# Block-sparse attention on one core: all steps in one hand-written order, sampled blocks from a packed table, V tiles held per pair, keys read in place

## The chip, the cores and the metric

The kernel runs on one core of a Trainium2 chip. The metric is device time of one execution, in microseconds (us). Engine names are those of the profile: PE is TensorE, PEld its weight loads, DVE is VectorE, ACT is ScalarE, POOL is GpSimd, SP is the engine whose queue issues all DMAs of this kernel.

## The reference

Attention over 4 batches of 8 heads, 768 positions of 64 numbers, with a mask in blocks of 32 positions (24 blocks), followed by a feed-forward layer with a clipped quadratic in place of a relu:

```python
scores = (1/sqrt(64)) * q @ k.T                  # per batch and head, 768 x 768
mask = |block(i) - block(j)| <= 1                # a band of three blocks
mask |= block(i) in (0, 23) | block(j) in (0, 23)    # first and last block see all and are seen by all
mask |= block(j) in sampled_blocks[block(i)]     # three blocks drawn per block of queries
attn = softmax(where(mask, scores, -1e9)) @ v
x = attn as (3072 tokens, 512)
h = x @ w_in                                     # 2048 columns
g = where(h >= 1, h, where(h <= -1, 0, (h + 1)**2 / 4))
out = g @ w_out
```

The sampled blocks are an input (64-bit integers), so which keys and values a block needs is known only on the chip. The two weights come as 64-bit floats and are converted on the chip.

## The kernel before

**Attention.** Two heads form a pair; there are 16 pairs, four for each batch. A pair has four rounds, a round eight blocks of queries. The first round scores the two global blocks (0 and 23) against all keys, the second adds the six blocks beside them, the third and fourth take eight blocks each. A block other than 0 and 23 needs 256 keys: the band of 96, the two global blocks (64), and three sampled ones (96). `gather_k` (L201) and `gather_k_sampled` (L212) copy these 256 columns of K into a tile `kg` on GpSimd: three wide copies a round for ends and bands, and one copy of 32 columns per sampled block (L218), 66 in a pair, each at an address from a register. `gather_v` (L221) does the same for V by DMA: three to four DMAs for the fixed blocks of each half of a round, and one DMA per sampled block (L240), again 66 in a pair, into a tile `vg`. The addresses come from two tables in SBUF (`k_at`, `v_at`); `offsets` (L113) reads the nine or twelve values that half a round needs into registers (L114), once on GpSimd for K and once on SP for V. A block that is sampled twice or already inside the band is pointed at 32 rows of zeros behind V.

**A round's steps.** `scores` (16 matmuls of 32 x 256, K of 64 rows, eight array tiles side by side), `top` (row maxima, DVE), `top_scale`, `expo` (ACT), `turn` (four transposes for each of the two heads, into one PSUM bank `t`), `turn_copy` (DVE for the first head, ACT for the second), `values` (16 matmuls of 128 rows x 32 for each head, 65 columns: 64 of V and a column of ones that sums the weights), `norm`. After the third and the fourth round three 128 x 128 tiles of the result are transposed (`x_turn`, L353) and split into a high and a low part (`x_hi`, `x_lo`). The round of the global blocks is scored first and finished inside the second one.

**Feed-forward.** `moe` (L398) works on 384 tokens, half a batch, at a time: 16 slices of 128 hidden columns each. A slice is 12 matmuls of 384 columns into the one bank `h` (`l1`, L421 to L423: three products of high and low parts for each of four pairs), then `g_relu`, `g_sq` (ACT), `g_max` (DVE), `g_hi` (ACT), `g_lo` (DVE), and nine matmuls of 512 columns (`l2`, L449 to L451). `h` is free for the next slice when `g_max` has read it. The second weight lies converted in DRAM and is loaded once per slice (L405). The feed-forward of batch b stands beside the attention of batch b + 1; that of the last batch has only its own tail beside it.

**Conversion.** `convert` turns 1 MB of 64-bit weights into two 32-bit parts: two DMAs into `raw`, one ACT and four DVE instructions on `cva`, then the split on ACT and DVE. Eight of these are needed for the first weight before the feed-forward can use it, eight more run during the first half-batch.

**Order.** Each step is entered into a list with a planned time (`at`); the list is sorted and called through at the end. Planned times are numbers in no unit that the chip knows: a pair of the first batch starts every `TP0` = 24 of them, a later one every `TP` = 48, a slice takes 6, and the table `P` holds how far before or after its round each step stands. The layer that records the instructions then lets an engine take instructions of different steps out of this order; so single matmuls of `values` stand between those of `l1` in the program. An engine runs its own instructions in the program's order. SP's DMAs stand in one queue, and each waits there until its target buffer is free.

```python
for k in range(n):
    for x in range(NR):
        Q_V.dma_start(out=vg[32 * x + 32:32 * x + 64, k0 + k, 1], in_=v_ext[b, j, bass.ds(at_[k * NR + x], BLK)])
```

## Time and profile before

| | |
|---|---|
| median of three runs | 1312.4 us (1311.61 to 1315.64) |
| profiled execution | 1320.8 us, of which the span of its instructions 1319.0 us |
| TensorE, matmuls | 1033.8 us busy (78%) |
| VectorE | 427.0 us (32%) |
| ScalarE | 412.4 us (31%) |
| GpSimd | 247.6 us (19%) |
| DMA | 157.89 MB in 155,837 packets, mean 120 GB/s |
| mean granted TensorE clock | 0.855 |

A matmul's busy time counts its way through the array, and matmuls follow each other before that ends, so 78% is not the share of TensorE's power that is used; what a stretch of matmuls costs is read from start to start. Issues of DMAs and register instructions are not counted as busy: SP has no row in the table, and its load is read from its queue.

### The profile page before, as it was taken

The page shows a single profiled execution, that of the slowest core. Times are in us where ns is not written, and L with a number is a line of the kernel's source. Part 1 is how long each engine was busy: PE and PEld are TensorE (multiplying, and loading weights), DVE is VectorE, ACT ScalarE, POOL GpSimd, SP SyncE. Part 2 cuts the span into 40 slices and gives each one's busy share as a digit, 9 for nine tenths or more (in the row PEclk, how much of TensorE's full clock was granted, in tenths as well). Part 3 has the DMA queues.
Part 4 walks back from the last instruction along what each step waited for, and adds up shares of the span by engine and source line. Part 5 has one row for each costly group of instructions (what it writes and reads, how often), then busy time and mean ns, then how long its engine had stood idle before and what let it go on. Part 6 is the DMA issues. An engine that isn't in the chain of part 4 may idle for free.

```text
span 1319.0 us, 26978 instructions
## 1 busy us (share of the span) xinstructions
PE 1033.8 (78%) x8928; PEld 742.6 (56%) x8928; DVE 427.0 (32%) x879; ACT 412.4 (31%) x800; POOL 247.6 (19%) x1205
## 2 busy tenths in 40 slices
...
GB/s 132 51 142 51 140 81 93 99 127 125 145 105 133 133 102 163 93 130 114 126 142 106 111 150 118 89 155 84 119 146 105 136 129 115 112 133 169 137 143 104
DMA packets 155837, 157.89 MB, mean 120 GB/s; under 512 B 25523, under 2 KB 128052, under 8 KB 155700
## 3 DMA queue, kind: packets, MB, share of 16 engines
...
q14 instruction: 65, 0.53, 0.1%
...
## 4 chain that ended last, share of the span: by engine, by line
SPq 44%; PE 29%; DMA 10%; issue 10%; DVE 4%; ACT 2%; POOL 1%; POOLq 0%; DVEq 0%; ACTq 0%
SPq L240 24%; SPq L114 10%; PE oa L449 5%; PE oa L450 4%; PE oa L451 4%; DMA w<-wo_dram 3%; PE h L421 3%; DMA raw<-in_moe_w_in_dram 3%; DMA vg<-in_v_ext_dram 3%; PE h L423 3%; PE h L422 3%; PE s L264 2%; SPq L231 2%; SPq L229 2%; SPq L234 2%
## 5 line engine op out<-in xcount | busy, mean ns | idle before, releaser
L421 PE MATMUL h<-x,wi 128*128 128x384 f32 x448 | 169.2, 378 | 59.1 <-DVE r L433 58.8
L218 POOL COPY kg<-k 128x32 f32 x1056 | 178.3, 222 | 124.9 <-issue 124.3
L449 PE MATMUL oa<-w,gh 128*128 128x512 f32 x384 | 166.5, 446 | 21.7 <-DMA w<-wo_dram 15.5
L319 PE MATMUL o<-vg,pt 128*32 128x65 f32 x2464 | 122.4, 256 | 66.6 <-DMA vg<-in_v_ext_dram 66.2
L76 ACT CAST gh<-r 128x384 fp32r<-128x384 f32 x128 | 65.6, 513 | 324.0 <-PE oa L450 298.7
L207 POOL COPY kg<-k 128x512 f32<-128x512 f32 (+1 forms) x48 | 29.1, 606 | 731.1 <-DMA k<-in_qk_t_dram 714.8
L450 PE MATMUL oa<-w,gh 128*128 128x512 f32 x384 | 162.5, 423 | 1.2 <-DVE w L161 1.2
L422 PE MATMUL h<-x,wi 128*128 128x384 f32 x448 | 161.5, 360 | 0.0
L451 PE MATMUL oa<-w,gl 128*128 128x512 f32 x384 | 161.1, 420 | 0.0
L423 PE MATMUL h<-x,wi 128*128 128x384 f32 x448 | 158.3, 353 | 0.0
L319 PEld LDWEIGHTS o<-vg,pt 128*32 128x32 f32 x2464 | 77.5, 127 | 134.0 <-issue 94.8
L421 PEld LDWEIGHTS h<-x,wi 128*128 128x128 f32 x448 | 87.4, 195 | 90.9 <-DVE r L433 77.2
L264 PE MATMUL s<-kg,q 64*32 64x256 f32 x1184 | 109.6, 430 | 30.7 <-POOL kg L218 15.0
L442 DVE TENSOR_TENSOR gl<-r,gh 128x384 fp32r<-128x384 f32 x128 | 71.4, 558 | 169.1 <-ACT gh L76 148.8
L433 DVE SCALAR_TENSOR_TENSOR r<-r,h 128x384 f32<-128x384 f32 x112 | 61.8, 552 | 162.2 <-ACT r L430 161.8
L301 PE MATMUL t<-idf,p 128*128 128x128 f32 x464 | 86.4, 312 | 32.9 <-DVE pt L305 11.8
L427 ACT ACTIVATE r<-h,half_c 128x384 f32<-128x384 f32 x112 | 65.1, 581 | 140.7 <-PE h L423 134.9
L449 PEld LDWEIGHTS oa<-w,gh 128*128 128x128 f32 x384 | 78.4, 207 | 46.8 <-DMA w<-wo_dram 20.9
L275 DVE TENSOR_REDUCE m<-s 128x2 f32<-128x512 f32 x80 | 53.6, 687 | 150.6 <-PE s L264 150.6
L301 PEld LDWEIGHTS t<-idf,p 128*128 128x128 f32 x464 | 59.8, 157 | 58.0 <-DVE pt L305 19.2
L422 PEld LDWEIGHTS h<-x,wi 128*128 128x128 f32 x448 | 88.0, 196 | 4.7
L450 PEld LDWEIGHTS oa<-w,gh 128*128 128x128 f32 x384 | 80.3, 209 | 17.9 <-DVE w L161 3.4
...
## 6 DMA issues: line engine op xcount, KB each, us to landing
w<-wo_dram SPq DMA_DIRECT2D x112, 512.0 KB, 3.6
vg<-in_v_ext_dram SPq DMA_DIRECT2D x1088, 16.2 KB, 1.7
...
vg<-in_v_ext_dram SPq DMA_DIRECT2D x128, 65.0 KB, 3.0
raw<-in_moe_w_in_dram SPq DMA_DIRECT2D x16, 512.0 KB, 4.8
raw<-in_moe_w_out_dram SPq DMA_DIRECT2D x16, 512.0 KB, 5.3
wo_dram<-w SPq DMA_DIRECT2D x16, 512.0 KB, 6.8
...
```

The source lines that it names most:

```text
L114: _, vals = nc.values_load_multi_w_load_instructions(table[:, i0 - 1:i0 - 1 + n].rearrange("a i r -> a (i r)"), engines=[engine], min_val= ...
L218: nc.gpsimd.tensor_copy(out=kg[:, k0 + k, 160 + 32 * a:192 + 32 * a], in_=kt[:, bass.ds(at_[k * NR + a], BLK)])
L240: Q_V.dma_start(out=vg[32 * x + 32:32 * x + 64, k0 + k, 1], in_=v_ext[b, j, bass.ds(at_[k * NR + x], BLK)])
L264: nc.tensor.matmul(out=st["s", r, e][32 * w:32 * w + 32, 256 * g:256 * g + 256], lhsT=st["q"][es, i * BLK:(i + 1) * BLK], rhs=rhs, start=T ...
L301: nc.tensor.transpose(out=t[:, c * 128:(c + 1) * 128], in_=st["p", r, e][:, c * 128:(c + 1) * 128], identity=idf)
L319: nc.tensor.matmul(out=o[32 * w:32 * w + 32, e, gd], lhsT=st["pt", r, e][:, k:k + 32], rhs=rhs, start=start, stop=stop)
L421: nc.tensor.matmul(out=hv, lhsT=wi[:, j, 0, fs], rhs=x[:, 0], start=(j == 0), stop=False)
L422: nc.tensor.matmul(out=hv, lhsT=wi[:, j, 0, fs], rhs=x[:, 1], start=False, stop=False)
L423: nc.tensor.matmul(out=hv, lhsT=wi[:, j, 1, fs], rhs=x[:, 0], start=False, stop=(j == NP - 1))
L449: nc.tensor.matmul(out=o, lhsT=gh[:, ts], rhs=w[:, 0], start=(fi == 0), stop=False)
L450: nc.tensor.matmul(out=o, lhsT=gh[:, ts], rhs=w[:, 1], start=False, stop=False)
L451: nc.tensor.matmul(out=o, lhsT=gl[:, ts], rhs=w[:, 0], start=False, stop=(fi == NF - 1))
```

## The change

- **Table.** The three sampled blocks of a query block are packed into one number of 15 bits (`pack`, `kv_at`). Each engine that needs it reads it once for the whole kernel (`blocks`: 22 values on SP, 22 on VectorE, 44 on GpSimd) and keeps it in registers; a field is taken out by register arithmetic at each use (`field`). `offsets` goes.
- **V.** Per pair a tile `va` holds the band and one global block for every query block, loaded by five DMAs (`load_va`); it serves all rounds. The second half of the 256 rows is `vb`, per round: two or three DMAs for the other global block, and the sampled blocks. Of the three sampled blocks the first is fetched by a DMA on SP and the other two are copied from `va` by GpSimd (`gather_v_sampled`); in the first batch's first three rounds SP fetches two and GpSimd copies one.
- **K.** Band and ends are no longer copied. `scores` reads them in place, with three matmuls of 96, 64 and 96 columns per query block and head where there was one of 256. Only the sampled 96 columns are gathered into `kg`; for the first batch's first three rounds most of these copies stand on VectorE.
- **Order.** The list is recorded under `manual_schedule`, so an engine's instructions stand in the order of the list. The tables of numbers are new. Of the first batch only the first three rounds stand ahead of the feed-forward; its fourth rounds load q, k and `va` again and stand behind the first slices. A conversion's load stands behind the start of the conversion before it. Transposes of results are moved to gaps of the bank `t` (`plan_turns`).
- **Buffers.** `raw`, `cva` and `vn` have one buffer instead of two, `gh` and `gl` two instead of three; results are stored per 128 tokens. The round's results have tiles of their own (`x1` to `x3`) in place of `xn`.

SP's instructions inside one later pair, before. `vg` is the V tile of a round, `w` the second weight, `ISA` a register instruction.

```order
L229 DMA vg<-in_v_ext_dram 96x4x130
L231 DMA vg<-in_v_ext_dram 32x4x130
L234 DMA vg<-in_v_ext_dram 32x4x130
L114 TENSOR_LOAD v_at
L240 ISA
L240 DMA vg<-in_v_ext_dram 32x130
```

The last two rows follow each other twelve times before SP comes to the next DMA. The same engine at the same place of the program now:

```order
L240 DMA va<-in_v_ext_dram 32x25x130
L241 DMA va<-in_v_ext_dram 32x22x130
L242 DMA va<-in_v_ext_dram 32x22x130
L243 DMA va<-in_v_ext_dram 32x21x130
L244 DMA va<-in_v_ext_dram 32x130
L250 DMA vb<-in_v_ext_dram 32x4x130 x2
L264 REGISTER_ALU
L264 ISA
L264 DMA vb<-in_v_ext_dram 32x130
```

The last three follow each other eight times for a whole round; there is no table read. In the whole program the DMAs of sampled blocks fall from 1056 to 408, and 464 register instructions on SP are new.

TensorE at a later round, before (`s` is the bank of the scores, `t` that of the transposes, `o` that of the values, `h` and `oa` those of the feed-forward):

```order
L301 MATMUL t<-idf,p 128x128 x4
L423 MATMUL h<-x,wi 128x384
L421 MATMUL h<-x,wi 128x384
L319 MATMUL o<-vg,pt 32x65 x4
L422 MATMUL h<-x,wi 128x384
L423 MATMUL h<-x,wi 128x384
L264 MATMUL s<-k,q 32x256 x7
L421 MATMUL h<-x,wi 128x384
```

A round's matmuls stood in several pieces between those of a slice. Now (L298 are the scores):

```order
L502 MATMUL oa_9892<-w,gl 128x512
L298 MATMUL s<-k,q 32x96 x8
L298 MATMUL s<-k,q 32x64 x8
L298 MATMUL s<-kg,q 32x96 x8
```

The three rows of scores come twice, 48 matmuls in one piece, and behind them three or six matmuls of one slice and twelve of the next; then the transposes and the values of that round (L335, L353):

```order
L335 MATMUL t<-idf,p 128x128 x4
L500 MATMUL oa_9892<-w,gh 128x512
L501 MATMUL oa_9892<-w,gh 128x512
L502 MATMUL oa_9892<-w,gl 128x512
L335 MATMUL t<-idf,p 128x128 x4
L500 MATMUL oa_9952<-w,gh 128x512
L501 MATMUL oa_9952<-w,gh 128x512
L502 MATMUL oa_9952<-w,gl 128x512
L353 MATMUL o<-va,pt 32x65 x4
L353 MATMUL o<-vb,pt 32x65 x4
```

Between two groups of transposes stand three matmuls of a slice, mostly; each head's 16 values stand in one piece. In the whole program TensorE changes from one kind of work to another 722 times instead of 882.

GpSimd inside one round, before:

```order
L207 COPY kg<-k 128x8x64
L210 COPY kg<-k 128x4x96 x2
L114 TENSOR_LOAD k_at
L218 ISA
L218 COPY kg<-k 128x32
```

and now, where the K copies of a round end and its V copies begin:

```order
L231 REGISTER_ALU x2
L231 ISA
L231 COPY kg_2159<-k_2020 128x32
L231 ISA
L231 COPY kg_2159<-k_2020 128x32
L266 REGISTER_ALU x2
L266 ISA
L266 COPY vb_2156<-va_2081 32x130
```

The wide copies and the table read are gone; a round has up to 24 copies of K and 16 of V, which are new here.

The diff, cut to its core:

```diff
-    def offsets(table, i0, n, engine, top):
-        _, vals = nc.values_load_multi_w_load_instructions(
-            table[:, i0 - 1:i0 - 1 + n].rearrange("a i r -> a (i r)"), engines=[engine], min_val=0, max_val=top,
...
+    def pack(dst, t):
+        w = cst.tile([1, NI, 1], F32, name="packed", bufs=2)
+        nc.vector.scalar_tensor_tensor(out=w, in0=t[:, :, 2:3], scalar=32.0, in1=t[:, :, 1:2], op0=ALU.mult, op1=ALU.add)
+        nc.vector.scalar_tensor_tensor(out=dst, in0=w, scalar=32.0, in1=t[:, :, 0:1], op0=ALU.mult, op1=ALU.add)
...
+    def blocks(engine, which, i):
+        if engine not in held:
+            rows = [1] if engine is ENG.SP else [0] if engine is ENG.DVE else [0, 1]
+            held[engine] = {}
+            for w in rows:
+                for i0 in range(0, NI, 11):
+                    _, vals = nc.values_load_multi_w_load_instructions(
+                        kv_at[:, i0:i0 + 11, w], engines=[engine], min_val=0, max_val=2 ** 15 - 1,
...
+        return held[engine][which, i]
+    def field(v, a, top):
+        return nc.s_assert_within((v >> (5 * a)) & 31 if a < NR - 1 else v >> (5 * a), 0, top,
...
-            st["raw"] = cv.tile([128, 1024, 2], I32, name="raw", bufs=2)
+            st["raw"] = cv.tile([128, 1024, 2], I32, name="raw", bufs=RAWB)
...
-        def gather_k(r):
...
-            nc.gpsimd.tensor_copy(out=kg[:, 0:total, 96:160].rearrange("p n (a c) -> p n a c", a=2), in_=ends)
...
+        def gather_k_sampled(r):
+            kg, kt = gat.tile([128, 8, BLK * NR], F32, name="kg"), st["k"]
...
+                for k in range(n):
+                    eng, et = (nc.vector, ENG.DVE) if wide and k in KD else (nc.gpsimd, ENG.Pool)
+                    v = blocks(et, 0, i0 + k)
+                    for a in range(NR):
+                        eng.tensor_copy(out=kg[:, k0 + k, 32 * a:32 * a + 32],
+                                        in_=kt[:, bass.ds(field(v, a, NB - 1) * BLK, BLK)])
...
+        def load_va():
+            va = st["va"] = gat.tile([128, NB + 1, VROW], F32, name="va", bufs=2)
+            Q_V.dma_start(out=va[32:64], in_=rows(0, BLK, NB + 1, BLK))
+            Q_V.dma_start(out=va[0:32, 1:NB - 1], in_=rows(0, BLK, NI, BLK))
+            Q_V.dma_start(out=va[64:96, 1:NB - 1], in_=rows(2 * BLK, BLK, NI, BLK))
+            Q_V.dma_start(out=va[96:128, 2:NB - 1], in_=rows(0, BLK, NI - 1, 0))
+            Q_V.dma_start(out=va[96:128, 1:2], in_=rows(S, BLK, 1, 0))
...
+        def gather_v_sampled(r, engine):
...
+                        if (a in (V_SPW if wide else V_SP)) is not (engine is ENG.SP):
+                            continue
+                        v = field(blocks(engine, 1, i0 + k), a, NB)
+                        dst = vb[32 * a + 32:32 * a + 64, k0 + k]
+                        if engine is ENG.SP:
+                            Q_V.dma_start(out=dst, in_=v_ext[b, j, bass.ds(v * BLK, BLK)])
+                        else:
+                            nc.gpsimd.tensor_copy(out=dst, in_=st["va"][32:64, bass.ds(v, 1)].rearrange("p a d -> p (a d)"))
...
+                for n in range(3 if r else 1):
+                    for w in range(4):
...
+                            c0, c1 = (0, 96, 160, 256)[n:n + 2]
...
+                            elif n == 0:
+                                rhs = kt[es, (i - 1) * BLK:(i + 2) * BLK]
...
+                            nc.tensor.matmul(out=st["s", r, e][32 * w:32 * w + 32, 256 * g + c0:256 * g + c1],
+                                             lhsT=st["q"][es, i * BLK:(i + 1) * BLK], rhs=rhs, start=True, stop=True)
...
+            if b == 0:
+                pair(b, j, j * TP0, TP0 / 3, True, (0, 1, 2))
+                pair(b, j, t0 + GAP + j * TP3, 0, False, (3,))
...
-    for _, fn, args in plan:
-        fn(*args)
+    with tc.manual_schedule():
+        for _, fn, args in plan:
+            fn(*args)
...
-P = {'lq': 40, 'lk': 40, 'lv': 30, 'gk': 20, 'gs': 19, 'gv': 25, 'sc': 0.6, 'sm': 0.7, 'ex': 2.2, 'e1': 0.8, 'e0': 0.4, 'tr': 4.0, 'tc': 5.0,
...
-TP0, TP = 24.0, 48.0
+TP0, TP1, TP, TP3, TPM = 18.214, 31.0, 48.427, 13.092, 64.075
+V_SP = (0,)
+V_SPW = (0, 1)
+VBUFS = 3
+RAWB, CVAB = 1, 1
+TCOPYW = (0, 1)
```

## Rows read from the trace of the kernel before

**Rows 1.** The page's part on the chain of work that ended last, followed back from the end: shares of the span by engine, then by engine and line (a q behind an engine's name is its sequencer or queue).

```profile
SPq 44%; PE 29%; DMA 10%; issue 10%; DVE 4%; ACT 2%; POOL 1%; POOLq 0%; DVEq 0%; ACTq 0%
SPq L240 24%; SPq L114 10%; PE oa L449 5%; PE oa L450 4%; PE oa L451 4%; DMA w<-wo_dram 3%; PE h L421 3%; DMA raw<-in_moe_w_in_dram 3%; DMA vg<-in_v_ext_dram 3%; PE h L423 3%; PE h L422 3%; PE s L264 2%; SPq L231 2%; SPq L229 2%; SPq L234 2%
```

**Rows 2.** Busy time by stretch of the span: start and end, length, then per engine busy us and (x instructions), the mean granted TensorE clock (1.00 is 2.4 GHz, 0.50 is 1.2 GHz), the share of the DMA engines and GB/s.

```profile
0.00:262.00 262.00, 144.04 (x1589) 75.44 (x1597) 99.33 (x198) 62.07 (x112) 78.35 (x364) 0.63 0.38 99
262.00:1170.00 908.00, 747.17 (x6627) 541.11 (x6611) 289.39 (x610) 293.44 (x581) 169.23 (x842) 0.90 0.42 121
1170.00:1319.00 149.00, 142.62 (x720) 126.04 (x720) 38.27 (x71) 56.94 (x107) 0.00 (x0) 0.98 0.44 147
1190.00:1290.00 100.00, 100.00 (x499) 90.11 (x498) 26.51 (x48) 40.48 (x77) 0.00 (x0) 1.00 0.44 146
```

**Rows 3.** Two views by line: all table reads and all V gathers on the SP queue (minimum, median and maximum ns of one, first and last start in us).

```profile
L114 SPq TENSOR_LOAD <-v_at x96: 746/2467/4519, 8.0 to 1161.7; - x96
...
L240 SPq DMA_DIRECT2D vg<-in_v_ext_dram x1056: 315/316/1683, 9.2 to 1170.0; - x176
```

**Rows 4.** The SP queue in order of time, inside one pair: start us, us, line, operation, out<-in, count of merged rows.

```profile
578.54 0.41 SPq L229 DMA_DIRECT2D vg<-in_v_ext_dram  x1
579.01 0.47 SPq L231 DMA_DIRECT2D vg<-in_v_ext_dram  x1
...
582.67 5.95 SPq L240 DMA_DIRECT2D vg<-in_v_ext_dram  x12
```

**Rows 5.** TensorE in order of time, inside the same pair: start us, us, line, operation, out<-in, tile, count, and in brackets the idle time before it and what ended it.

```profile
560.17 0.34 PE L423 MATMUL h<-x,wi 128*128 128x384 f32 x1
560.36 0.34 PE L421 MATMUL h<-x,wi 128*128 128x384 f32 x1
560.62 0.30 PE L319 MATMUL o<-vg,pt 128*32 128x65 f32 x2
560.86 0.44 PE L422 MATMUL h<-x,wi 128*128 128x384 f32 x1
...
566.96 0.89 PE L319 MATMUL o<-vg,pt 128*32 128x65 f32 x48
...
578.75 0.60 PE L301 MATMUL t<-idf,p 128*128 128x128 f32 x4
579.10 0.42 PE L422 MATMUL h<-x,wi 128*128 128x384 f32 x1
...
590.28 1.93 PE L264 MATMUL s<-kg,q 64*32 64x256 f32 x16 [4.32 <-ACT p L295]
```

**Rows 6.** Busy time by stretch again (columns as in the second group): the 65 us up to a fall of the granted clock, the fall, and the 64 us behind it.

```profile
525.00:590.00 65.00, 53.41 (x496) 39.35 (x495) 20.21 (x44) 22.11 (x45) 12.09 (x59) 1.00 0.38 101
590.00:597.00 7.00, 6.72 (x65) 4.62 (x66) 1.46 (x4) 0.79 (x2) 2.64 (x18) 0.53 0.77 276
597.00:661.00 64.00, 54.34 (x514) 39.45 (x512) 20.14 (x45) 24.29 (x49) 11.65 (x56) 1.00 0.41 112
```

**Rows 7.** GpSimd in order of time in the same pair (columns as for TensorE; "issue" is time in which it waited for nothing but its own sequencer).

```profile
578.22 0.61 POOL L207 COPY kg<-k 128x512 f32<-128x512 f32 x1
...
580.50 1.86 POOL L218 COPY kg<-k 128x32 f32 x12 [0.77 <-issue]
584.61 1.86 POOL L218 COPY kg<-k 128x32 f32 x12 [2.25 <-issue]
```

**Rows 8.** Groups by line: line, engine, operation, out<-in and shapes, count | busy us, mean ns of one | idle us before them and what ended it.

```profile
L442 DVE TENSOR_TENSOR gl<-r,gh 128x384 fp32r<-128x384 f32 x128 | 71.4, 558 | 169.1 <-ACT gh L76 148.8 <-PE t L353 19.7
L430 ACT ACTIVATE r<-r 128x384 f32<-128x384 f32 x128 | 67.0, 524 | 3.3
L295 ACT ACTIVATE p<-s,m 128x256 f32<-128x256 f32 x160 | 66.1, 471 | 61.8 <-DVE m L287 51.8 <-PE t L301 4.5 <-PE h L301 3.6
L76 ACT CAST gh<-r 128x384 fp32r<-128x384 f32 x128 | 65.6, 513 | 324.0 <-PE oa L450 298.7 <-DVE r L433 24.6
L427 ACT ACTIVATE r<-h,half_c 128x384 f32<-128x384 f32 x112 | 65.1, 581 | 140.7 <-PE h L423 134.9 <-DVE gl L442 4.6
L433 DVE SCALAR_TENSOR_TENSOR r<-r,h 128x384 f32<-128x384 f32 x112 | 61.8, 552 | 162.2 <-ACT r L430 161.8
...
L275 DVE TENSOR_REDUCE m<-s 128x2 f32<-128x512 f32 x80 | 53.6, 687 | 150.6 <-PE s L264 150.6
...
L305 DVE COPY pt<-t 128x512 f32<-128x512 f32 x60 | 41.4, 690 | 106.6 <-PE t L301 54.3 <-PE o L319 39.9 <-PE oa L319 12.4
...
L305 ACT COPY pt<-t 128x512 f32<-128x512 f32 x56 | 32.7, 585 | 90.2 <-PE t L301 49.1 <-PE o L319 23.2 <-PE oa L319 17.8
```

**Rows 9.** Busy time of the instructions that read or write the tile cva (the 64-bit weights' conversion; 16 of them in the span) on VectorE and ScalarE.

```profile
0.00:1319.00 1319.00, 81.79 (x88) 35.75 (x40) 0.86 0.42 120
```

**Rows 10.** TensorE at the first matmul of the feed-forward part and at the last of the span (columns as above).

```profile
275.19 0.69 PE L421 MATMUL h<-x,wi 128*128 128x384 f32 x1
...
1314.62 0.39 PE L451 MATMUL oa<-w,gl 128*128 128x512 f32 x1
```

**Rows 11.** DMA issues by line: out<-in, queue, operation, count, KB each, median us from issue to landing.

```profile
vg<-in_v_ext_dram SPq DMA_DIRECT2D x1088, 16.2 KB, 1.7
...
raw<-in_moe_w_in_dram SPq DMA_DIRECT2D x16, 512.0 KB, 4.8
...
k<-in_qk_t_dram SPq DMA_DIRECT2D x16, 384.0 KB, 5.6
```

238 lines of the change are left out of this document (119 added, 119 removed).

## Prediction

> **What bounds the kernel now.** I began with the chain of work that ended last [rows 1]. SP's queue holds 44% of it, TensorE 29%. Within SP two lines carry it: the V gathers of sampled blocks (24%) and the table reads (10%). Next, the busy time by stretch [rows 2] cuts the span in three: up to 262 us the attention of the first batch, to 1170 us twelve pairs beside the feed-forward, 75.7 us each (908 / 12), and a tail of feed-forward alone. In the tail TensorE is busy all the time at clock 1.00 and does 499 matmuls in 100 us; in the twelve pairs no engine that computes is full.
>
> The queue itself shows why [rows 3, 4]. Twelve gathers of one block take 5.95 us, 0.50 each with their register work; another DMA takes about 0.41, 0.47 with what lies between two; a table read of twelve values 2.47 us, 0.206 a value. A pair has 66 gathers (33 us), 66 values (13.6 us), some 23 other DMAs for q, k and V (11 us) and eight loads of w (3 us): 61 of its 75.7 us are SP's own work, most of the rest are waits of the w loads in the same queue. TensorE waits for it: 4.32 us ahead of a score block [rows 5], and with each such wait the granted clock falls, 0.53 over the next 7 us and 1.00 on either side [rows 6].
>
> **The change part by part.**
>
> *SP.* Gathers fall from 1056 to 408, the 96 reads with 1056 values to 22 values. With some 340 other DMAs at 0.47, 112 w loads at 0.41, the gathers at 0.53 and 4.5 us for the table, SP has 216 + 160 + 46 + 5 = 427 us of work in all. Of the gathers' 0.53, 0.03 is my estimate for a register instruction more; no row shows that kind. Its ends: nothing, and 0.206 us, what a table value costs; the 168 in the beginning would then add 30 us. In a later pair SP has 22 gathers, 15 other DMAs and eight w loads, 22 us: no longer the bound.
>
> *Beginning.* Ahead of the feed-forward stand three rounds of each of four pairs. SP per pair: 28 gathers (14.8 us), 13 other DMAs (6.1), four halves of weights (1.9), 22.8 us. The table can be read from about 8.0 us [rows 3], plus 0.4 for two DVE instructions more, and takes 4.5. Four pairs make 91, of which 7 stand ahead of the table; behind the last gather come landing (1.7 us [rows 11]), values, normalizing and transposes, about 5: 8.4 + 4.5 + 91 - 7 + 5 = 102. VectorE has per pair two conversions (81.79 / 16 = 5.1 each [rows 9]), six maxima at 0.69 [rows 8], 36 K copies that are new there, and some 3.6 of small ones. A 32-column copy on VectorE has no row; between 0.155 (GpSimd's pace [rows 7]) and 0.69 (512 columns [rows 8]) I take 0.2, near the lower one. That is 25 us per pair, and 8.4 + 4.5 + 100 = 113, of which the last part lies behind the first feed-forward matmul. I take 107 for the start of the feed-forward, 275 us before [rows 10]. Low end 95; high end 150, from 0.69 a copy (+18 a pair on VectorE, partly beside waits) or from the single buffer of `raw`: a conversion is then landing (4.8 [rows 11]) plus 7.3 us of VectorE and ScalarE in turn ([rows 9], both engines over 16), and SP stands at the next load with the gathers queued behind it.
>
> *TensorE behind that.* It is the bound, as I read the rest. The feed-forward has 2688 matmuls at 0.2004 us: 539 us. A score block of 16 takes 1.93 us at clock 0.53, so 1.0 at full. Into 48 matmuls go the same columns. Low end: no more than now. High end: the time goes by matmuls, 0.064 each, 3.1. The nearest row is 48 value matmuls in 0.89 us [rows 5], 0.0185 each with their weight loads, which can run under eight array tiles' work: I take 1.2. Going from feed-forward to small matmuls and back costs 0.3 (two values between two feed-forward matmuls move the second 0.50 us on, 0.19 is its own pace), 0.25 for scores. Four transposes take 0.35 to the next feed-forward matmul, I take 0.45 with the switch to values; three transposes of results the same. A pair: first scores 1.25, three blocks at 1.45, eight groups and two of results at 0.45, two blocks of 24 values at 0.74 and four of 16 at 0.6: 14.0 us, 168 for twelve. Four rounds left over from the first batch: 1.45 + 0.9 + 1.2 + 0.45 = 4.0 each, 16. In all 723 us.
>
> The Trainium skill's TensorEngine Tiling (Array Packing), section Instruction Overhead, speaks against the split: it gives each matmul an overhead of about 60 cycles. At 2.4 GHz that would be an estimated 25 ns for each of 32 more, 0.8 us a block; with it the sum would be 24 us higher over 40 blocks. The row of 48 matmuls in 0.89 us leaves no room for that much per matmul on top of their work.
>
> *Waits of TensorE.* The four transposes of one head wait until the bank `t` is copied out: 0.69 on VectorE or 0.59 on ScalarE [rows 8] and some 0.2 of handing over, and in the new order only three matmuls (0.5 to 0.7 us) stand between most groups: 0.2 x 45, and six groups of eight at 0.85: 14 us. From scores to transposes: two maxima (1.29 together), scale 0.17, two exponentials at 0.47, 0.2 of handing over, 2.6; the order puts 2.3 to 4.2 us of feed-forward there, enough when both engines are free. A slice's chain to the next (0.58 + 0.52 + 0.55 [rows 8], some 0.25 of handing over, 1.9) lies under nine matmuls, 2.08. ScalarE and VectorE work 293 and 289 us in the twelve pairs of now [rows 2], 24 each per pair, and a pair is to take about 50: a step finds its engine taken half the time, for half an operation of 0.55. Five steps in each of 52 rounds and three in each of 97 slices, half of them covered, make 551 x 0.5 x 0.27 x 0.5 = 37. Together 50 us. Low end 10, as the tail runs without a gap; high end under the rivals. Since no wait is then near 4 us I leave the clock at 1.00.
>
> *The first half-batch* carries eight conversions (41 us on VectorE), 16 slices at 1.11 [rows 8] and nine rounds, some 31: 90 of VectorE beside 67 + 31 = 98 of TensorE. Two engines as full as that wait for each other; I add 10 (0 to 20).
>
> *GpSimd.* The wide copies go (0.61 for 512 columns) and the reads between copies (2.25 us idle [rows 7]). A copy takes 0.155 with 32 columns; between these two rows 130 columns come to 0.25, so 44 V copies are 11 us and 66 K copies 10.2, register work mostly beside them: 22 to 28 us a pair. Hidden under TensorE's 47.
>
> *Ends.* Single buffers of `vn`, `gh`, `gl`, smaller stores: nothing, hidden by slices of 4.2 us; half a slice (2 us) once per pair if not, 24. From the last matmul to the end of the span 4 us (1314.62 to 1319.0 [rows 10]), and 2 outside.
>
> Sum: 107 + 723 + 50 + 10 + 4 + 2 = 896 us against the profiled 1320.8. The runs' median is 0.6% below that execution, so 890.
>
> **The rivals.**
>
> *Slower: gathering and computing in turn.* SP waits in order for buffers that TensorE frees, GpSimd for SP, TensorE for GpSimd. If no pair's gather ran ahead of the one before, a pair would be k's landing (5.6 [rows 11]), 22 on GpSimd, 22 on SP, 47 on TensorE: 97 us, and 107 + 16 + 12 x 97 + 31 slices of 4.2 + 6, 1420 us. It decides from 89 us a pair. Against it: `va`, q, k and `kg` have two buffers, `vb` three, and loads stand a third of a pair ahead. That SP would still bind, the change not doing what it says, is excluded by 427 us of work against 890.
>
> *Waits not covered.* If engines find each other late in most rounds, another 40 us and, with gaps like that of 4.32 us, a fall of the clock per pair as now (7 us at half pace, 3.5 lost, 42 in all): 972. For it: a fixed order can't take other work. Against it: 24 us of ScalarE and VectorE work in 50.
>
> *Long beginning*, by conversions: 150 instead of 107, 933.
>
> *Scores by matmul count*, 3.1 instead of 1.2 in 40 blocks: 76 more, 966.
>
> *Nearly all covered:* waits and half-batch cost 10 instead of 60, beginning 100: 833.
>
> **How the numbers follow.** Forecast 0.56, its own range 845 (beginning 95, waits 25, scores nothing more) to 945 (beginning 125, waits 87); waits 0.15; beginning 0.10; scores 0.05; covered 0.10; slower 0.03, and 0.01 for a mixture that ends near 1312. The range, 820 to 985, takes in the likely part of all but the slower one. What a measurement here can tell from no change is about 0.3%: faster 0.96, same 0.01, slower 0.03.
>
> **What would show it right or wrong.** In the profile after, the first feed-forward matmul near 107 us; SP's gathers and table reads gone from the chain, TensorE first in it; stretches of a pair at 55 us or less with the clock at 1.00; six rows of eight score matmuls starting within 1.4 us; GpSimd under 30 us a pair; VectorE near full only up to some 215 us. I am wrong if the twelve pairs are above 65 us each, if idle time of GpSimd or SP still ends TensorE's waits, or if the clock falls once a pair.

## The result and the profile after

The changed kernel takes 1016.6 us (median of four runs, 1013.6 to 1019.2) where the kernel before takes 1312.1 on the same chip: a ratio of 0.774, 95% interval 0.772 to 0.777. The forecast was 890 and its range ended at 985. The sign and most of the size came, 296 us of 422; 127 us did not.

The chain that ended last, by engine and by line, as in [rows 1]:

```profile
PE 63%; DVE 13%; DMA 8%; ACT 7%; issue 4%; SPq 3%; DVEq 1%; ACTq 0%
PE oa L500 8%; PE h L472 8%; PE oa L501 7%; PE oa L502 7%; PE h L474 6%; PE h L473 6%; PE o L353 6%; PE s L298 6%; PE t L335 5%; DMA raw<-in_moe_w_out_dram 3%; DVE m L309 3%; DMA raw<-in_moe_w_in_dram 3%; ACT p L329 2%; DVE pt L339 2%; SPq 
```

SP's 44% are 3%, TensorE's 29% are 63%. The rows by stretch (columns as in [rows 2]) show where the new span is good and where it is not:

```profile
0.00:176.00 176.00, 69.67 (x1740) 50.58 (x1740) 99.70 (x299) 54.22 (x94) 32.97 (x128) 0.73 0.66 155
176.00:331.00 155.00, 115.00 (x1627) 93.68 (x1628) 80.61 (x149) 61.82 (x120) 88.25 (x314) 0.87 0.78 196
...
338.00:1009.00 671.00, 646.48 (x8513) 541.44 (x8493) 253.34 (x564) 290.52 (x588) 259.92 (x1102) 1.00 0.52 145
```

From 338 us to the last matmul TensorE is busy 646 of 671 us and its clock is 1.00. Ahead of that, two stretches that the forecast put at 107 and 108 us take 176 and some 160. Two instructions mark their ends: the first feed-forward matmul on TensorE (275.19 in [rows 10]), and the first copy of a finished result on ScalarE (tile `ot`), which comes when sixteen slices are done.

```profile
176.08 0.69 PE L472 MATMUL h<-xt,wi 128*128 128x384 f32 x1 [8.49 <-DVE xt L393]
```

```profile
L509 ACT COPY ot<-oa x23: 567/587/604, 337.6 to 1010.2; 128x512 f32<-128x512 f32 x23
```

| part of the sum | forecast | measured | from |
|---|---|---|---|
| beginning, to the first feed-forward matmul | 107 | 176.1 | row above |
| first half-batch, to the first `ot` | 67 + 31 + 10 = 108 | 161.5 | 337.6 - 176.1 |
| the rest, to the last matmul | 896 - 107 - 108 - 4 - 2 = 675 | 671 | stretch above |
| end of the span, and outside | 6 | 8 | 1016.6 - 1008.8 |
| scaling of the profiled execution to the median | -6 | 0 | span 1014.0 |

So the steady part, two thirds of the time, came within 4 us, and the miss is 69 + 53 us in the first third, with 6 from a scaling that did not repeat. Most experiments ask what holds that third; r8 and r11 ask which part of the change brings what.

**The beginning in SP's queue.** This is one whole pair of the first batch, from one load of `va` to the next (columns as in [rows 4]):

```profile
81.67 0.36 SPq L240 DMA_DIRECT2D va<-in_v_ext_dram  x1
82.08 0.52 SPq L241 DMA_DIRECT2D va<-in_v_ext_dram  x1
82.65 0.51 SPq L242 DMA_DIRECT2D va<-in_v_ext_dram  x1
83.20 0.87 SPq L243 DMA_DIRECT2D va<-in_v_ext_dram  x1
84.11 2.70 SPq L244 DMA_DIRECT2D va<-in_v_ext_dram  x1
86.92 0.83 SPq L163 DMA_DIRECT2D raw<-in_moe_w_in_dram  x2
87.86 0.37 SPq L207 DMA_DIRECT2D k<-in_qk_t_dram  x1
88.33 0.41 SPq L207 DMA_DIRECT2D q<-in_qk_t_dram  x1
88.83 1.29 SPq L211 DMA_DIRECT2D vn<-in_v_ext_dram  x1
91.01 2.23 SPq L250 DMA_DIRECT2D vb<-in_v_ext_dram  x2
93.28 0.42 SPq L252 DMA_DIRECT2D vb<-in_v_ext_dram  x1
94.07 9.73 SPq L264 DMA_DIRECT2D vb<-in_v_ext_dram  x12
103.91 0.83 SPq L163 DMA_DIRECT2D raw<-in_moe_w_in_dram  x2
104.84 0.85 SPq L250 DMA_DIRECT2D vb<-in_v_ext_dram  x2
105.96 10.74 SPq L264 DMA_DIRECT2D vb<-in_v_ext_dram  x16
116.80 0.36 SPq L240 DMA_DIRECT2D va<-in_v_ext_dram  x1
...
154.34 0.36 SPq L240 DMA_DIRECT2D va<-in_v_ext_dram  x1
```

SP goes from one instruction to the next with hardly a pause: 35.1 us for this pair and 37.5 for the next, where I had 22.8. The 28 gathers take 20.7 (94.07 to 103.91 and 105.96 to 116.80), 0.74 each for my 0.53. The five loads of `va` take 5.25 for my 2.35, and the slowest is the last and by far the smallest, 32 rows for one block: it stands behind four loads of 670 to 800 rows each, and SP is held in it. What remains takes 9.2 for 5.6. Four such pairs put SP's last gather at 154 us in place of 97.

From there to the first feed-forward matmul it is another 22 us, not 10. The chain of waits shows why:

```profile
158.40 0.41 SPq L163
...
158.86 10.31 DMA raw<-in_moe_w_out_dram
...
169.27 1.13 ACT cva L170
...
174.36 1.20 DVE m L309 x2
175.56 0.47 DVE xt L393
```

The order by hand puts a conversion's load behind the gathers and the next `va`, and its first instruction on ScalarE and VectorE ahead of the last softmax and the last transposes of the pair. The load lands after 10.3 us, where the kernel before had 5.3 for these loads, and all that stands behind it in the order waits too:

```profile
raw<-in_moe_w_out_dram SPq DMA_DIRECT2D x16, 512.0 KB, 5.3
```

**The first half-batch** has the same event at a larger price. SP, ScalarE and VectorE around 240 us (idle time before an instruction and what ended it in brackets), and the stretch:

```profile
239.42 0.87 SPq L163 DMA_DIRECT2D raw<-in_moe_w_out_dram  x2
```

```profile
250.03 1.12 ACT L170 ACTIVATE cva<-raw 128x1024 f32<-128x1024 f32 x1 [12.79 <-DMA raw<-in_moe_w_out_dram]
251.05 0.57 ACT L478 ACTIVATE r<-h,half_c 128x384 f32<-128x384 f32 x1
```

```profile
251.18 0.69 DVE L171 TENSOR_SCALAR cva<-cva 128x1024 f32<-128x1024 f32 x1 [11.81 <-ACT cva L170]
...
255.51 0.54 DVE L484 SCALAR_TENSOR_TENSOR r<-r,h 128x384 f32<-128x384 f32 x1
```

```profile
238.00:256.00 18.00, 4.65 (x53) 3.77 (x45) 5.48 (x9) 2.38 (x4) 14.55 (x50) 0.74 0.86 229
```

Two engines stand 12 us for one load; the slice's steps (L478, L484) stand behind them, and TensorE works 4.65 of 18 us. The waits by line give "PE h L472 <- DVE r L484" 25.6 us in five waits for the stretch from 176 to 331.

### The profile page after: what moved, and what is told of

Its sections match the earlier page's. It is cut to its first block, busy times and chain, and to the rows that moved or that the text cites. A ratio compares the mean times of both kernels' runs of the same rounds, so it can differ in the third digit from the quotient of the medians.

```text
span 1014.0 us, 34082 instructions
## 1 busy us (share of the span) xinstructions
PE 837.8 (83%) x12000; PEld 691.2 (68%) x12000; DVE 435.8 (43%) x1013; ACT 411.8 (41%) x812; POOL 387.0 (38%) x1564
## 4 chain that ended last, share of the span: by engine, by line
PE 63%; DVE 13%; DMA 8%; ACT 7%; issue 4%; SPq 3%; DVEq 1%; ACTq 0%
PE oa L500 8%; PE h L472 8%; PE oa L501 7%; PE oa L502 7%; PE h L474 6%; PE h L473 6%; PE o L353 6%; PE s L298 6%; PE t L335 5%; DMA raw<-in_moe_w_out_dram 3%; DVE m L309 3%; DMA raw<-in_moe_w_in_dram 3%; ACT p L329 2%; DVE pt L339 2%; SPq L264 2%
## 5 line engine op out<-in xcount | busy, mean ns | idle before, releaser
L266 POOL COPY vb<-va 32x130 f32 x648 | 208.8, 326 | 162.5 <-DMA va<-in_v_ext_dram 102.4
L472 PE MATMUL h<-xt,wi 128*128 128x384 f32 x448 | 164.9, 368 | 38.1 <-DVE r L484 26.7
L500 PE MATMUL oa<-w,gh 128*128 128x512 f32 x384 | 163.8, 427 | 0.4 <-ACT gh L75 0.3
L474 PE MATMUL h<-xt,wi 128*128 128x384 f32 x448 | 154.1, 344 | 0.0
L473 PE MATMUL h<-xt,wi 128*128 128x384 f32 x448 | 154.0, 344 | 0.0
L502 PE MATMUL oa<-w,gl 128*128 128x512 f32 x384 | 152.8, 398 | 0.0
L501 PE MATMUL oa<-w,gh 128*128 128x512 f32 x384 | 152.2, 396 | 0.0
L478 ACT ACTIVATE r<-h,half_c 128x384 f32<-128x384 f32 x112 | 65.3, 583 | 164.5 <-PE h L474 164.0
L484 DVE SCALAR_TENSOR_TENSOR r<-r,h 128x384 f32<-128x384 f32 x112 | 61.7, 551 | 146.5 <-ACT r L481 146.3
L472 PEld LDWEIGHTS h<-xt,wi 128*128 128x128 f32 x448 | 86.9, 194 | 52.2 <-DVE r L484 31.5
L335 PE MATMUL t<-idf,p 128*128 128x128 f32 x464 | 78.2, 293 | 42.1 <-ACT p L326 18.5
L335 PEld LDWEIGHTS t<-idf,p 128*128 128x128 f32 x464 | 54.5, 147 | 70.3 <-ACT p L326 27.0
L329 ACT ACTIVATE p<-s,m 128x256 f32<-128x256 f32 x176 | 71.8, 473 | 62.4 <-DVE m L321 53.0
L473 PEld LDWEIGHTS h<-xt,wi 128*128 128x128 f32 x448 | 87.2, 195 | 4.6 <-issue 1.4
L474 PEld LDWEIGHTS h<-xt,wi 128*128 128x128 f32 x448 | 86.5, 193 | 0.0
L500 PEld LDWEIGHTS oa<-w,gh 128*128 128x128 f32 x384 | 72.9, 190 | 17.0 <-issue 3.9
L502 PEld LDWEIGHTS oa<-w,gl 128*128 128x128 f32 x384 | 72.6, 189 | 16.7 <-DVE gl L493 0.3
L298 PE MATMUL s<-k,q 64*32 64x96 f32 (+2 forms) x3376 | 72.8, 267 | 11.6 <-DMA q<-in_qk_t_dram 6.2
L501 PEld LDWEIGHTS oa<-w,gh 128*128 128x128 f32 x384 | 73.3, 191 | 6.6
```

Source lines behind the costliest of these rows:

```text
L266: nc.gpsimd.tensor_copy(out=dst, in_=st["va"][32:64, bass.ds(v, 1)].rearrange("p a d -> p (a d)"))
L298: nc.tensor.matmul(out=st["s", r, e][32 * w:32 * w + 32, 256 * g + c0:256 * g + c1], lhsT=st["q"][es, i * BLK:(i + 1) * BLK], rhs=rhs, sta ...
L329: nc.scalar.activation(out=p[:, 256 * g:256 * g + 256], in_=st["s", r, e][:, 256 * g:256 * g + 256], func=AF.Exp, bias=st["m", r][:, e, g: ...
L335: nc.tensor.transpose(out=t[:, c * 128:(c + 1) * 128], in_=st["p", r, e][:, c * 128:(c + 1) * 128], identity=idf)
L472: nc.tensor.matmul(out=hv, lhsT=wi[:, j, 0, fs], rhs=x[:, 0], start=(j == 0), stop=False)
L473: nc.tensor.matmul(out=hv, lhsT=wi[:, j, 0, fs], rhs=x[:, 1], start=False, stop=False)
```

## The experiments

All changes below are to the changed kernel, except r8. Times are medians; the ratio is to the kernel before on the same chip, with its 95% interval. "FF" is the first feed-forward matmul, "ot" the first result copy, "rest" from there to the last result copy, all from the traces, in us.

| run | edit | time | ratio | FF | ot - FF | rest |
|---|---|---|---|---|---|---|
| after | | 1016.6 | 0.774 (0.772-0.777) | 176 | 161 | 673 |
| r1 | four tiles with one buffer less | 1109.5 | 0.845 (0.842-0.848) | 175 | 169 | 760 |
| r2 | r1, `raw` twice, loads earlier | 1102.2 | 0.839 (0.837-0.842) | 165 | 175 | 762 |
| r3 | no conversions | 956.4 | 0.729 (0.725-0.733) | 142 | 141 | 671 |
| r4 | only the V rows needed | 997.2 | 0.760 (0.757-0.762) | 165 | 154 | 678 |
| r5 | one of three V blocks on SP | 985.1 | 0.752 (0.749-0.755) | 145 | 162 | 671 |
| r6 | three of three on SP | 1047.9 | 0.799 (0.796-0.802) | 209 | 163 | 671 |
| r7 | `raw` loaded by ScalarE's queue | 1045.0 | 0.798 (0.795-0.800) | 194 | 174 | 669 |
| r9 | r5, `raw` in halves | 988.7 | 0.753 (0.750-0.756) | 149 | 162 | 672 |
| r10 | r9 with r4 | 972.5 | 0.741 (0.737-0.744) | 146 | 150 | 672 |
| r11 | no order by hand | 1098.5 | 0.835 (0.830-0.841) | 168 | 224 | 702 |
| r12 | r5 without conversions | 927.6 | 0.707 (0.704-0.710) | 122 | 127 | 672 |
| r13 | none on SP | 989.5 | 0.751 (0.748-0.755) | 142 | 165 | 680 |
| r14 | r10, halves three times, earlier | 978.3 | 0.744 (0.740-0.747) | 145 | 152 | 678 |
| r15 | r14, none on SP | 985.6 | 0.750 (0.746-0.755) | 146 | 154 | 679 |
| r16 | r5, r4, K copies to GpSimd | 959.4 | 0.729 (0.726-0.732) | 131 | 151 | 672 |
| r17 | K copies to GpSimd alone | 1016.1 | 0.774 (0.771-0.777) | 176 | 162 | 672 |
| r18 | r16, halves three times, earlier | 963.7 | 0.732 (0.729-0.735) | 132 | 151 | 676 |

**Is it the single raw buffer?** A load waits for the last bits of the conversion before it, so load, landing and conversion could form a ring of 18 us, sixteen times. r1 only makes the room that r2's second buffer needs.

```diff
-    wst = pool("wst", 3)
+    wst = pool("wst", 2)
-XNBUFS = 5
+XNBUFS = 4
...
-            o = op.tile([128, DM], F32, name="ot", bufs=2)
+            o = op.tile([128, DM], F32, name="ot", bufs=1)
```

The third tile of `x3` goes too.

> The kernel after with less room: one buffer fewer for the tiles x1, x3, w and ot, nothing else. It is the control for the next run, which needs that room. All theories: within 10 us of the kernel after (1017), the first feed-forward matmul at 176 us as there; if w's third buffer matters, the later stretches lose some us each pair.

A miss: 93 us more, nearly all of it behind `ot`, in the part that has nothing to do with the question. In

```profile
345.00:1101.00 756.00, 673.85 (x8513) 558.17 (x8493) 252.19 (x563) 290.55 (x588) 257.48 (x1100) 0.95 0.47 129
```

the same 8513 matmuls leave TensorE idle for 82 us and not 25, and the clock falls to 0.95 with the gaps. I did not try which of the four tiles it is; its waits name the result's store, w's landing and the K copies behind the scores.

```diff
-RAWB, CVAB = 1, 1
+RAWB, CVAB = 2, 1
...
-            at(max(t - P["cl"], prev + 0.1), load)
-            prev = t
+            at(max(t - P["cl"], older + 0.1), load)
+            older, prev = prev, t
```

> The control with two buffers for raw, each conversion's load standing one conversion earlier in the order. Ring theory (queue, landing and arithmetic of a conversion come in turn because raw has one buffer, 18.4 us each, sixteen times, up to 313 us): the first feed-forward matmul falls from 176 to 120 to 140, the sixteen slices behind it from 155 to about 115, the time from 1017 to about 940. DMA theory (the DMA engines, 0.66 and 0.76 busy in these stretches, are the limit): their share rises little and the time stays within 20 us of the control. SP theory (the queue is full of gathers): first matmul not before 160, time down by 20 at most.

7 us less than r1; FF comes 10 us earlier, `ot` 4. The second buffer did its work: ScalarE's waits for `raw` in the first 340 us come to 3.5 us, where r1 has 42.8 and the changed kernel 66.7. So the ring is not what holds the beginning.

**How much do conversions and V's loads cost?**

```diff
-            nc.scalar.activation(out=f(a), in_=f(hi32), func=AF.Abs)
...
+            st["a"] = fixed_a
```

> Leaves out the loads of the 64-bit weights and the five instructions that convert them (the split reads a constant tile, so the weights are not the inputs'); the rest of the order is unchanged. It shows what is left of the beginning without conversions. Ring theory: the first feed-forward matmul at 105 to 120 us, sixteen slices in 105 to 115, time 1017 - 100 = about 910, all behind that as in the kernel after. SP theory: first matmul at 150 or later, as the gathers still fill the queue. DMA theory: the 17 MB less of 62 MB in the first 357 us give 95 us, so about 920, but then the next run must gain too.

60 us less, 34 of them before FF and 21 in the half-batch. FF at 142 lies between what the two theories gave, so the conversions hold the beginning in part, and something else holds it too.

```diff
-            Q_V.dma_start(out=va[0:32, 1:NB - 1], in_=rows(0, BLK, NI, BLK))
...
+            for lo, hi in ((1, 12), (20, 23)) if wide else ((12, 20),) if rounds == (3,) else ((1, 23),):
+                Q_V.dma_start(out=va[0:32, lo:hi], in_=rows((lo - 1) * BLK, BLK, hi - lo, BLK))
```

> The kernel after, with the band and global rows of va loaded only for the query blocks whose rounds use them: 1.1 MB in place of 1.5 MB for each pair's first three rounds (three DMAs more), 0.8 MB in place of 1.5 MB for the fourth rounds of the first batch; 4.4 MB less of 62 MB in the first 357 us, nearly all in 520-byte packets, which are more than half of the DMA engines' time there. DMA theory: 25 us less or more. Ring theory: within 10 us of 1017, as the loads of raw land little sooner. SP theory: 4 to 6 us slower by the three DMAs.

19 us less, though SP issues more DMAs: 221 ahead of FF in 165 us, where 209 took 176. The DMA theory gave at least 25, the SP theory a loss, so neither came as put. What fell is SP's stay in a DMA and the landings: the last load of `va`, which moves one block as before, holds SP for 0.43 us in the median (1.69 in the changed kernel), and the loads of the first weight land after 5.3 (6.2). How the gain divides between the two is not shown.

**Is it SP's issue?** r5 and r6 change one number in opposite directions. In the traces that moves 56 of SP's 408 gathers each way, all ahead of FF (the expectations count 60, those of r12 and r13 wrongly 84).

```diff
-V_SPW = (0, 1)
+V_SPW = (0,)
```

> The changed kernel with one number changed: in the first batch's wide pairs one of the three sampled V blocks of a query block is fetched by SP and two are copied by GpSimd (it is two and one in the changed kernel). SP loses 60 of the 120 gathers that stand ahead of the first feed-forward matmul. Theory 'SP's issue binds the beginning' (209 DMAs fill 176 us, a gather costs 0.63 to 0.83 of it): first feed-forward matmul 38 to 50 us earlier, at 126 to 140, all together 950 to 980. Rival 'the chain of conversions with one raw buffer binds it' (16 conversions of 18 to 19 us each, to 313 us): little change, 1000 to 1016.

```diff
-V_SPW = (0, 1)
+V_SPW = (0, 1, 2)
```

> The changed kernel with the opposite change: all three sampled V blocks of a query block in the wide pairs are fetched by SP, none copied by GpSimd. SP's issue: 60 gathers more ahead of the first feed-forward matmul, 38 to 50 us later, at 214 to 226, and 30 to 40 gathers more in the rest of the first batch: 1060 to 1100 all together. Conversions: their cycle grows only by the gathers in front of a load (6 x 0.65 = 4 us in each of 9 cycles), 1030 to 1050 at most.

31.5 us less and 31.3 more, 0.56 a gather both times, and all of it before FF:

```profile
145.04 0.69 PE L472 MATMUL h<-xt,wi 128*128 128x384 f32 x1 [4.54 <-DVE xt L393]
```

```profile
208.50 0.69 PE L472 MATMUL h<-xt,wi 128*128 128x384 f32 x1 [14.58 <-DVE xt L393]
```

SP's issue is a bound of the beginning: the effect has the same size in both directions, and r5 left the range of its rival (1000 to 1016). It came short of the 38 to 50 that I had expected from 0.63 to 0.83 a gather, and r6's 1047.9 also lies in the range that its expectation gave the conversions (1030 to 1050). I take it that a gather costs its own issue there, and that the waits among the gathers stay when gathers go; no run shows that by itself.

```diff
-    Q_RAW = nc.sync
+    Q_RAW = nc.scalar
```

> The changed kernel with the loads of the raw weights issued by ScalarE's queue and not by SP's. SP loses 32 DMAs of 0.4 us and their waits (13 us of issue, 11 us of waits for the raw buffer), and a load no longer stands behind 12 to 16 gathers. SP's issue: 10 to 25 us shorter, 990 to 1005. Conversions: a cycle of 18 to 19 loses its 3 to 7 us in the queue, 5 x 16 = 80 us shorter, 935 to 950.

28 us more, against both theories. The loads leave SP, but on ScalarE each stands in front of the softmax until VectorE has finished the conversion before:

```profile
L163 ACTq EVENT_SEMAPHORE  x15: 1530/5315/16539, 11.4 to 311.8; - x15
```

Fifteen waits, 5.3 us in the median and 16.5 at most (minimum, median, maximum in ns), with everything of ScalarE behind them. The Trainium skill's DMA: Bandwidth & Descriptors, section Issuing engines are not separate DMA queues, says that issuing from several engines saves only the sequencer's time, usually small beside the DMA itself. r5 and r6 show that here it was not small (0.56 us a gather, 31 us for 56 of them), and r7 that a queue is no gain where its engine has other work behind the wait.

**Which part of the change brings what?** r8 is the kernel before with the packed table alone, r11 the changed kernel without the order by hand.

```diff
-                at_ = offsets(v_at, i0, n, ENG.SP, S)
...
-                        Q_V.dma_start(out=vg[32 * x + 32:32 * x + 64, k0 + k, 1], in_=v_ext[b, j, bass.ds(at_[k * NR + x], BLK)])
+                        Q_V.dma_start(out=vg[32 * x + 32:32 * x + 64, k0 + k, 1], in_=v_ext[b, j, bass.ds(field(blocks(ENG.SP, 1, i0 + k), x, NB) * BLK, BLK)])
```

> The kernel before with one part of the change alone: the packed table, read once into registers of SP and GpSimd; gathers, order of the work and block-wise sums stay as before. Theory 'SP's issue bound the kernel before': SP loses 16 x 13.6 us of table reads, and its 1056 gathers cost 0.10 to 0.16 more each for the register work (0.60 to 0.66 where it was 0.50): 217 less and 106 to 169 more, so 1200 to 1265. Rival 'the reads were hidden': within 10 us of 1312.

1253.4 us, ratio 0.954 (0.950 to 0.958): 57 us less, inside the expected span. Twelve gathers that took 5.95 in [rows 4] take a microsecond more with the register work:

```profile
619.60 6.95 SPq L257 DMA_DIRECT2D vg<-in_v_ext_dram  x12
```

```diff
-    with tc.manual_schedule():
-        for _, fn, args in plan:
-            fn(*args)
+    for _, fn, args in plan:
+        fn(*args)
```

> The changed kernel with the hand-written order switched off: the same instructions, handed over in the same sequence, with each engine's order left to the language's own scheduling, as in the kernel before. If the order by hand carries little, and the packed table, the V tiles per pair and the keys read in place carry the gain: 1000 to 1040. If the order carries the cover of softmax and of the V and K copies under the feed-forward: 1080 to 1250.

1098.5: the order by hand is worth 82 us; by the traces 54 lie ahead of `ot` and 29 behind it. Of the 296 us, the other 214 come from the rest of the change together: the table, V's tiles, keys in place, buffers and the new list. Of these only the table has a run of its own.

**What binds once SP is eased?**

```diff
-                st["raw"] = cv.tile([128, 1024, 2], I32, name="raw", bufs=RAWB)
+                st["raw", k] = cv.tile([128, 512, 2], I32, name="raw", bufs=2)
```

> As r5 (one of three sampled V blocks of the wide pairs on SP), and the raw weights in two half tiles of 4 KB a row, two buffers, converted half by half, where one tile of 8 KB had one buffer: the next load starts when the first half of the last conversion is done. Theory 'with SP eased the ring of the single raw buffer is the bound' (in r5 SP stands 0 to 0.1 us after the last bits at 9 of 15 loads, and a cycle is 15 us: 8 landing, 7 converting): a cycle 2 to 4 us shorter, 16 cycles, so 30 to 60 us less than r5's 985, 925 to 955. Rival 'SP still binds': within 8 of 985.

Nothing (988.7 beside r5's 985.1). r10 adds r4's edit:

> r9, and of V's neighbour blocks only those loaded that a pair uses, as in r4. If the packets of these loads hold SP and the landings (r4: 19 us less), 10 to 25 us less than r9; if the ring or TensorE is all that binds by then, within 5 of r9.

16 us less than r9, 12 of them in the half-batch. r12 is r5 with r3's edit:

> r5 without the conversions of the weights, which are left out as in r3 (a constant tile takes the place of the loaded words). If SP's issue binds r3's beginning too (142 us for 176 DMAs), 84 gathers fewer take another 25 to 35 us: 922 to 935, first feed-forward matmul near 110. If without conversions it is the chain of scores, softmax, copies and values that binds the beginning, 945 to 960.

927.6, where the SP theory had it: 29 us under r3 and 57.5 under r5. Gathers and conversions are two prices that add up. FF at 122 and `ot` at 249.6 (127 us) are the nearest that any run came to the forecast's 107 and 108.

```diff
-V_SPW = (0, 1)
+V_SPW = ()
```

> The changed kernel with all three sampled V blocks of the wide pairs copied by GpSimd, none fetched by SP there. If SP's issue is still the bound after r5, another 84 gathers fewer take 25 to 35 us more: 950 to 960, first feed-forward matmul near 115. If after r5 the ring of the raw buffer is the bound (load, landing, conversion: 15 us each, 16 times), the last conversion ends at 275 to 285 as in r5 (282.8) and the time stays at 975 to 990.

No further gain (989.5), so SP is the bound only down to about r5's number of gathers. The time lies where the expectation put it for the ring, and SP now stands 53.9 us at the load of `raw` (of 142), until the conversion before it is done. r9 had already split that buffer and gained nothing; r15 below eases both at once.

```profile
SPq L163 <- DVE cva L176: 53.9, 8, 9.6
```

```diff
-            at(max(t - P["cl"], prev + 0.1), load)
+            at(max(t - P["cl"], older + 0.2), load, 0)
+            at(max(t - P["cl"], prev + 0.1), load, 1)
...
-VBUFS = 3
+VBUFS = 2
```

> r10 (one block on SP, needed V rows only, half tiles) with three half tiles for the raw weights, and half of each load placed one conversion earlier in the order; the room for the third comes from VBUFS, 3 to 2. Ring theory: half a landing, 4 us, less in each of 16 cycles, 30 to 50 us off the beginning and the first half-batch against r10 (first feed-forward matmul 146, first sixteen slices done at 289): 105 to 130 and 240 to 260. SP theory: those two times as in r10, within 6 us. The two buffers for V tiles show apart from this in the later pairs, 51.5 us each with three; I expect 51 to 56.

> r14 with no sampled V block of the wide pairs on SP. If SP and the ring each hold the beginning when the other is eased, this is the shortest: first feed-forward matmul at 95 to 115, first sixteen slices done at 215 to 240, all together 905 to 940 with later pairs of 51.5 us. If neither does (VectorE, or GpSimd's copies, 0.33 us each, which come in turn with TensorE's rounds), within 8 us of r14.

Both a little worse than r10. They are not clean: the V tile that gave the room is waited for too (SP 24.2 us in four waits on "PE o L356"). r18 repeats the test further on, with VectorE eased.

```diff
-KD = (0, 1, 2, 4)
+KD = ()
```

> The changed kernel with one sampled V block on SP (r5), the needed V rows only (r4), and all sampled K blocks of the wide pairs copied by GpSimd, where VectorE copies four query blocks' of each eight (KD empty). Without the last I expect 965 to 975 (r10 was 972.5 with half tiles, which gave nothing in r9). Theory 'with SP eased VectorE, 73% busy up to 130 us with 25 us of copies and 10 of idle time between them, binds the beginning': 15 to 30 less, 940 to 955, first feed-forward matmul at 118 to 130. Rival 'the chain of one round after the other binds it': 962 to 975.

> The changed kernel with KD empty alone: VectorE loses its K copies in the wide pairs, GpSimd gets them, SP is as before. If SP's issue is the bound of the changed kernel and VectorE only the one behind it: 1008 to 1020, first feed-forward matmul at 170 to 178. If VectorE held it too: 985 to 1000.

With SP as it was, taking 25 us of K copies from VectorE gives nothing (1016.1); with SP eased it gives up to 13 (959.4 beside r10's 972.5), a little under what I expected. r10 has half tiles too, which cost 3.6 in r9 beside r5, so the copies alone may be worth 9. So VectorE stands behind SP as a bound, not beside it. r16 is the shortest of the runs that compute everything: 5.6% under the changed kernel, with two numbers and V's load loop changed.

> r16 with the three half tiles for the raw weights, half of each load one conversion earlier, and two V tiles in place of three (r14's change). In r16 SP stands at the load when the last bits are done (0 to 0.1 us behind them at 9 of 15), so with SP and VectorE both eased the ring should hold at last: a cycle of 13 to 15 us shorter by 2 to 4, first feed-forward matmul at 105 to 122 (131 in r16), 5 us given back in the four left-over rounds as in r14: 925 to 950. If the order of the steps, not the buffer, holds the cycle: within 8 of 959.

No gain (963.7). In its trace SP issues half a load at 66.71, and ScalarE takes it up at 85.63:

```profile
66.71 0.35 SPq L163 DMA_DIRECT2D raw<-in_moe_w_in_dram  x1
```

```profile
85.63 1.25 ACT L170 ACTIVATE cva<-raw 128x512 f32<-128x512 f32 x2
```

ScalarE comes to it from other work, without a wait for the data; up to FF it waits for `raw` only twice, 4.4 us in all. The conversion's turn in ScalarE's and VectorE's order holds it there. With r2 and r9, the ring is excluded. What holds FF at 131 in r16, where GpSimd is busy 95 of the first 130 us and the other engines that compute less, stays open; I take it for the chain of one round after the other with conversions between, but no run took that apart.

## Why the prediction was right or wrong

**Right: what bounded the kernel before, and what would after.** SP fell out of the chain and TensorE took its place; r8 shows the table reads as a cost of their own. The rest of 675 us came as 671. A pair in steady state takes 51.9 us (first scores of the rounds at 457.7 and, seven pairs on, 820.9), the clock stays at 1.00, and GpSimd is busy some 26 us a pair, inside my 22 to 28. The rivals of gathering and computing in turn, of waits not covered and of scores by matmul count fall with these rows. The copy of 32 columns on VectorE was 0.186 us in the mean for my 0.2. A copy of 32 x 130 on GpSimd was 0.326 for my 0.25, without effect.

**Right in the sum, not in its parts: TensorE behind the beginning.** I had 50 us of waits; TensorE is idle 24.5 us of the 671, so its work is some 22 us longer than I made it. That the two cancel to 4 us is luck. The prices, from rows of the trace:

```profile
560.33 0.40 PE L502 MATMUL oa<-w,gl 128*128 128x512 f32 x1
560.65 0.65 PE L298 MATMUL s<-k,q 64*32 64x96 f32 x35
...
561.95 0.50 PE L500 MATMUL oa<-w,gh 128*128 128x512 f32 x1
...
581.71 0.40 PE L502 MATMUL oa<-w,gl 128*128 128x512 f32 x1
582.29 0.63 PE L335 MATMUL t<-idf,p 128*128 128x128 f32 x4 [0.18 <-ACT r L481]
582.67 0.47 PE L500 MATMUL oa<-w,gh 128*128 128x512 f32 x1
```

A score block moves the next feed-forward matmul 1.62 us on, 0.23 of it that stream's own pace: 1.39, where I had 1.45 with the switch. A group of four transposes moves it 0.96 on, 0.73 more than its own pace and 0.18 of that a wait: 0.55 for my 0.45. That is the price behind a wait; in the seven pairs from 457.7 to 820.9 groups without one take 0.36, so 0.45 was near the middle.

I also read one row wrongly: the trace has two records for each matmul of scores and values, 96 for this block of 48. So the sixteen records of [rows 5] were half a round and not a whole one, and its 48 records of values were 24 matmuls. A whole old round, 32 records, is this line in the chain of the kernel before (start, us, engine, tile, line, records; the clock is 1.00 there):

```profile
427.07 1.02 PE s L264 x32
```

Elsewhere it stood in two pieces, 0.98 and 0.58 us (338.19 and 341.94). The split round takes 1.30 from its first record to the next feed-forward matmul (560.65 to 561.95), more than an old round in one piece and less than one in two; so the split was not cheaper in itself. My 1.2 was near by luck: in both rows behind it I took records for matmuls. The values show the error: in the seven pairs 24 of them move the next feed-forward matmul 1.13 on for my 0.74, 16 of them 0.69 to 0.90 for my 0.60. That is 14 to 17 us in twelve pairs; scores and the transposes of results came some 8 us below my prices, and the rest of the 22 no row takes apart.

The Trainium skill's TensorEngine Tiling (Array Packing), section Instruction Overhead, gives about 60 cycles a matmul, an estimated 25 ns at 2.4 GHz. The trace does not contradict that: 1.30 us are 27 ns for each of the 48 matmuls. The prediction's row that left no room for it counted records; by matmuls it has 37 ns each. What did not come is the 0.8 us a block that the prediction worked out from it: with the old 1.0 and the switch of 0.25 that would be 2.05, and 1.39 were measured.

**Wrong: the beginning, step "SP per pair: 28 gathers (14.8 us), 13 other DMAs (6.1), four halves of weights (1.9), 22.8 us".** That SP issues its way through the beginning was right (r5 and r6); the term was mis-sized: 35 to 37 us a pair. Three prices were too low. A gather was 0.53, with 0.03 for one register instruction more; that is 0.08 (5.95 to 6.95 for twelve in r8), and r5 and r6 give 0.56 for the gather. But I had nothing for waits on earlier DMAs, which stand among the gathers (7.6 us in the two pairs from 81.67 to 154.34) and bring them to 0.74. A load of `va` was priced at 0.47 like any DMA; five take 5.25 a pair, because SP stays in the instruction while the loads ahead of it are large. And the loads land later beside each other: `raw` after 6.2 us for the first weight and 8.4 for the second in the median, where the kernel before had 4.8 and 5.3.

```profile
va<-in_v_ext_dram SPq DMA_DIRECT2D x40, 357.5 KB, 8.2
raw<-in_moe_w_in_dram SPq DMA_DIRECT2D x16, 512.0 KB, 6.2
raw<-in_moe_w_out_dram SPq DMA_DIRECT2D x16, 512.0 KB, 8.4
```

The prediction had SP at 102 us and VectorE at 113 and took 107 between them. r17 takes the K copies from VectorE and gains nothing, and VectorE, which I had near full up to 215 us, is busy 99.7 of the first 176; r5 and r6 put the price on SP. My high end of 150 was made from VectorE's copies and from the raw buffer. The 30 us that I named as the upper end of SP's register work did not go into it; they were made from 168 gathers, and four pairs of 28 are 112. The rival "long beginning" had the right place and part of the cause: r3 puts 34 us ahead of FF on the conversions, but r2 and r9 show that it is not the single buffer.

**Wrong: "Two engines as full as that wait for each other; I add 10 (0 to 20)".** The half-batch lost 53 us. This is the stretch in the changed kernel and in r12 (columns as in [rows 2]):

```profile
176.08:337.60 161.52, 121.25 (x1737) 98.79 (x1738) 82.37 (x151) 66.11 (x130) 93.71 (x334) 0.88 0.79 198
...
122.40:249.60 127.20, 114.24 (x1737) 92.69 (x1738) 56.50 (x123) 59.16 (x123) 82.88 (x337) 0.96 0.83 187
```

I had 98 us of work for TensorE and 10 of waits. It is idle for 40 us, so 30 of the 53 are waits; the other 23 are work that took longer, at a granted clock of 0.88 where I had left it at 1.00. Without conversions (r12) 13 us of idle time remain.

I looked at how full VectorE and TensorE are, 90 and 98 us, and not at what stands at the head of VectorE's order: a conversion that waits for a load, which waits in SP's queue behind V's loads. r12 against r5 puts 35 us on the conversions there (162 to 127), r3 against the changed kernel 21, r4 some 8 on V's loads. In [rows 9] I had their work, 82 us in all; their waits had no term. That the wait for the load is what costs, and not the conversion's place in the order, is read from the 12.8 us above and not isolated: r2 takes nearly all waits for `raw` away, and its half-batch is no shorter (175 us, r1 has 169).
